# Attention backward loop: one transposing transfer per block of four units in place of two

## The chip, the cores and the metric

The kernel runs on one core of a Trainium2 chip. A core has engines that run side by side, each with its own in-order instruction stream: PE (TensorE, matmuls; PEld is its weight load), DVE (VectorE), ACT (ScalarE), POOL (GpSimd) and SP (SyncE, used here only to issue DMA transfers). They meet through semaphores. Sixteen DMA engines move data for all of them. The metric is the device time of one execution in microseconds (us).

## The reference

The kernel computes a transformer block with adaptive layer norm, forward and backward: the output and nine gradients, for 2048 tokens of width 512, in bfloat16. Forward, attention has 32 heads of 16 columns. Cut to what matters here:

```python
x = A_x
h = _layernorm(x) * (1 + ca) + sa
scores = einsum('bhqd,bhkd->bhqk', q, k) * Dh ** (-0.5)
p = softmax(scores);  o = einsum('bhqk,bhkd->bhqd', p, v)
x = x + ga * (o @ wo)
...
_out, _vjp = jax.vjp(_f, A_x, A_wqkv, A_wo, ...)
_grads = _vjp(grad_out)
```

The change lies in the backward pass of the attention. For a head, with E the exponentials of the scores and dO the gradient of o, it needs dS = E * (dO V^T - row term), and from it dK (dS transposed times Q), dV (E transposed times dO) and dQ (dS times K). As dS stands, with 128 queries on the partitions, PE can contract it over queries for dK. For dQ it must contract over keys, and for that dS has to be transposed.

## The kernel before

The program has three phases: the forward pass with the dense layers (to about 1115 us of the profile), the attention backward loop (to about 2388 us), and the input gradients and weight gradients (to the end). The change touches only the loop.

**Units and blocks.** A unit is four heads (head group hg, 8 of them) by 512 keys (kc, 4) by 128 queries (qc and qi, 4 by 4): `units`, line 1554, 512 in all. Four units that differ only in qi form a block, of which there are 128; block b holds units 4b to 4b+3. A head group has 16 blocks.

**What is done for a unit.** `score` (line 1587): four matmuls, one for each head, into one of three score banks of PSUM (A, B, C). `expo` (1597): four exponentials on ACT, from the banks into tile E_u. `dp_pair` (1602), twice: two matmuls into psD_u, then one DVE product (1616) that writes half of the unit's dS. `k_quad` (1648) and `v_quad` (1657): four matmuls each for dK and dV. `transpose_unit` (1623) issues the transposing transfers of dS from SP.

**What is done for a block.** Tile dsT holds the block's dS transposed, [128 keys, 4 units, 16 tiles, 128 queries]. `dq_quad` (1673, matmuls on line 1681) reads it, four times for a block, each over all four units at once; then `dq_out` (1684) evicts and adds up dQ.

**Two kinds of blocks.** In an even block all four units are transposed by DMA. In an odd block (`on_pe`, 1620) the fourth unit is transposed by PE (`pe_turn`, 1640, line 1644) and copied into dsT by ACT (1760), and only three go by DMA.

**Tiles and buffers.** A dS tile holds two units and has four buffers (1608, `cur["dS"]`); dsT has three buffers (1549). The tile framework puts in the waits: a new tile waits until the old one in its buffer has been read. A transfer reads 0.5 MB for each unit. In `transpose_unit` an even block makes two transfers of two units each, after its second and after its fourth unit (line 1631); an odd block makes one of two units after its second (1631), and one of one unit after its third (1629).

**The order.** It is written out by hand: in every round b the tokens of `order_t` (1705) or `order_n` (1710) are issued to the engines, and each engine follows that order. In round b: "s" and "e" are scores and exponentials of block b; "D" is a `dp_pair`, which runs one block behind or less: a block's fourth unit is finished by the first D that does work in the round after its own; "q" the dK and dV matmuls; "t" and "T" the PE transposes and copies of block b-1; "d1" and "d2" the `dq_quad`s of block b-2, in the second half of the round; "Q" its `dq_out`. A transposing transfer is issued right behind the D that completes its last unit. `order_t` runs when block b-1 is odd.

**Queues.** In the loop SP issues the transposing transfers, and in the last head group also five loads of 512 KB for the next phase (`load_grads`, 1546). ACT issues the loads for the next head group and the stores of finished gradients (`load`, 1576), one every four D's: 22 loads for each head group, and the stores. SP and ACT transfers draw their completion semaphores from the same eight. After the loop SP goes on with the loads of the last phase (1778 and after).

```python
            elif qi % 2 == 1:
                SP.dma_start(out=dqt[u // 4][:, qi - 1:qi + 1].rearrange("p u b q -> p (u b) q"),
                             in_=cur["dS"].rearrange("p u h k -> p (u h k)"), transpose=True)
```

Of the kernel before, what the change touches and what calls it, by code (L numbers as in the profile page):

```python
# [17 lines left out]
BF = dt.bfloat16  # L18
F32 = dt.float32

P = 128
# [13 lines left out]
def kernel(  # L35
# [21 lines left out]
    SP = nc.sync  # L57
# [89 lines left out]
    with ExitStack() as ph:  # L147
# [4 lines left out]
        ework = att.enter_context(tc.tile_pool(name="phCe", bufs=4))  # L152
# [1393 lines left out]
        SP.dma_start(out=tile_ap, in_=(dQc if key == "dq" else dVKtP)[i])  # L1546

    with ExitStack() as ph:
        tpool = ph.enter_context(tc.tile_pool(name="phIt", bufs=3))
        ework = ph.enter_context(tc.tile_pool(name="phIe", bufs=4))  # L1550
        wk = ph.enter_context(tc.tile_pool(name="phIw", bufs=2))
        psd = ph.enter_context(tc.tile_pool(name="psId", bufs=2, space=bass.MemoryType.PSUM))
# [3 lines left out]
        hst, bst, sst, dqt, cur = {}, {}, {}, {}, {}  # L1556
# [45 lines left out]
        def dp_pair(u, pair):  # L1602
            hg, kc, qc, qi = units[u]
            st = hst[hg]
            qt = qc * 4 + qi
            if pair == 0:
                if qi % 2 == 0:
                    cur["dS"] = ework.tile([P, 2, 4, 512], BF, name="dS_u", tag="dS_u", bufs=4)
                bst[u][1] = cur["dS"][:, qi % 2]
            E_u, dS_u = bst[u]  # L1610
            psD = psd.tile([P, 2, 512], F32, name="psD_u", tag="pd")
            for hi in range(2):
                r = 32 * (2 * pair + hi)
                PE.matmul(psD[:, hi, :], st["do"][r:r + 32, qt * P:(qt + 1) * P], st["v"][r:r + 32, kc * 512:kc * 512 + 512],  # L1614
                          start=True, stop=True, tile_position=(r, 0))
            DVE.tensor_tensor(dS_u[:, 2 * pair:2 * pair + 2, :], psD[:], E_u[:, 2 * pair:2 * pair + 2, :], ALU.mult)  # L1616
            if qi == 3 and on_pe(u // 4):
                held["dS"] = dS_u

        def on_pe(b):  # L1620
            return b % 2 == 1

        def transpose_unit(u):
            hg, kc, qc, qi = units[u]
            if qi == 0:
                dqt[u // 4] = tpool.tile([P, 4, 16, P], BF, name="dsT", tag="dsT")
            if on_pe(u // 4) and qi >= 2:
                if qi == 2:
                    SP.dma_start(out=dqt[u // 4][:, qi], in_=bst[u][1].rearrange("p h k -> p (h k)"), transpose=True)
            elif qi % 2 == 1:  # L1630
                SP.dma_start(out=dqt[u // 4][:, qi - 1:qi + 1].rearrange("p u b q -> p (u b) q"),
                             in_=cur["dS"].rearrange("p u h k -> p (u h k)"), transpose=True)

        held = {}

# [84 lines left out]
        with tc.manual_schedule(engines={PE.engine, ACT.engine, DVE.engine, SP.engine, POOL.engine}):  # L1720
# [4 lines left out]
            for b in range(NU // 4 + 3):  # L1725
                toks, bank = order_t if on_pe(b - 1) else order_n
                for tok in toks:
# [12 lines left out]
                    elif c == "D":  # L1740
                        if 0 <= nD < 2 * NU:
                            dp_pair(nD // 2, nD % 2)
                            if nD % 2 == 1:
                                transpose_unit(nD // 2)
                        nD += 1
                        cur["j"] = nD
                        for j in sorted(j for j in todo if j <= nD):
                            for f, args in todo.pop(j):
                                f(*args)
                    elif c == "q":  # L1750
                        if 0 <= nq < 2 * NU:
                            (v_quad if nq % 2 else k_quad)(nq // 2)
                        nq += 1
                    elif c == "f" and 0 < nq < 2 * NU:
                        keep_warm()
                    elif c == "t" and 0 <= b - 1 < NU // 4:
                        pe_turn(b - 1, i - 1)
                    elif c == "T" and 0 <= b - 1 < NU // 4:
                        dst, pt = held.pop(i - 1)
                        ACT.activation(dst, pt[:], AF.Identity)  # L1760
                    elif c == "d" and 0 <= b - 2 < NU // 4:
                        for kt in (2 * i - 2, 2 * i - 1):
                            dq_quad(b - 2, kt)
                    elif c == "Q" and 0 <= b - 2 < NU // 4:
                        dq_out(b - 2)
# [3 lines left out]
    with ExitStack() as ph:  # L1769
# [139 lines left out]
        with tc.manual_schedule(engines={PE.engine, ACT.engine, DVE.engine}):  # L1909
# [33 lines left out]
            for b in range(3):  # L1943
                for ic in range(DC):
# [8 lines left out]
                    elif i <= 2 * DC:  # L1953
                        k, h = (i - 1) // 2, (i - 1) % 2
# [67 lines left out]
```

## Time and profile before

| | |
|---|---|
| time, median of 3 runs | 2492.1 us (2487.35, 2492.10, 2492.11) |
| profiled execution, span | 2501.3 us |
| backward loop in it | about 1115 to 2388 us, 128 blocks |
| DVE product for dS, line 1616 | 1024 x 1.218 us |
| ACT exponential, line 1600 | 2048, some 0.65 us each, started every 0.48 us |
| transposing issue of two units, line 1631 | 192 |
| transposing issue of one unit, line 1629 | 64 |
| share of SP's DMA queue (q1) in the bytes moved | 389.35 of 437.70 MB |

How to read it: the busy rows say how much of the span each engine worked. The page cuts the span into 40 slices of 62.5 us and gives a digit for tenths busy. PEclk is the clock granted to TensorE, in tenths of full speed. The stretches view gives the same for any window, with the number of instructions in brackets. Its DMA share is a sum over packets, which overlap, and so can be above 1. In the view by tile a row gives the shortest, median and longest duration in ns and the first and last start in us. A row on "SPq" is SP's queue issuing a transfer; its duration is the time that SP is held by the issue, not the time until the data has landed. In the chain of waits a row gives start, duration and what the chain ran through; "DMA out<-in" there runs from the issue to the semaphore that released the waiting engine. Lines of the timeline that are alike and follow each other closely are merged (x3), with their whole extent as duration.

### The profile page before, as it was taken

To read this page: it belongs to the slowest core of one execution; us is meant where nothing else is said; L and a number is where in the kernel's file an instruction comes from. 1 tells how busy PE (TensorE), PEld (TensorE's weight loads), DVE (VectorE), ACT (ScalarE), POOL (GpSimd) and SP (SyncE) were. 2 spreads that over 40 slices of the span, in tenths; PEclk is the share of its full clock that TensorE was granted. 3 is DMA by queue.
4 is the path that set the end of the run, shared out by engine and by line. 5 is a ranking of instruction groups with operands and counts; after the bars stand their busy time and mean duration, and the time that the engine had idled before them with its cause. 6 is when DMAs were issued, how large, how long until landed. Compare 5 with 4: busy or idle time off the path is not lost.

```text
span 2501.3 us, 49888 instructions
## 1 busy us (share of the span) xinstructions
PE 2324.0 (93%) x18948; PEld 783.4 (31%) x19036; DVE 1837.7 (73%) x2377; ACT 2303.7 (92%) x3560; POOL 488.0 (20%) x661
## 2 busy tenths in 40 slices
PE   8899899989998998999999999999999999999989
PEld 3232233223332333443223323233232323332344
DVE  6555354455435444579989999999999999999965
ACT  7999999999998999539999999999999999999944
POOL 2111223323533453110111101111011110110100
PEclk9999999999998999999999999999999999999999
DMA  4468463258546865979999999999999999999984
GB/s 146 130 167 176 144 150 97 88 166 142 98 95 142 151 131 110 256 200 196 201 192 206 199 198 202 196 204 203 205 205 198 205 202 199 200 198 214 201 253 133
DMA packets 1189503, 437.70 MB, mean 175 GB/s; under 512 B 1065867, under 2 KB 1160521, under 8 KB 1188878
## 3 DMA queue, kind: packets, MB, share of 16 engines
q1 hardware_dynamic: 1152414, 389.35, 79.0%
q0 software_dynamic: 19872, 27.09, 6.5%
q10 hardware_dynamic: 16976, 18.07, 2.9%
q8 instruction: 149, 2.44, 0.4%
q14 instruction: 92, 0.75, 0.1%
HBM read 98.30 MB, written 70.80 MB: 68 GB/s over the span
## 4 chain that ended last, share of the span: by engine, by line
ACT 40%; PE 38%; issue 8%; DVE 7%; DMA 3%; SPq 1%; ACTq 1%; POOL 0%; DVEq 0%; another core or an unknown queue 0%; POOLq 0%
ACT E_u L1600 24%; ACT ET L578 12%; PE dqacc L1681 4%; PE psST L576 3%; PE psS_A L1594 3%; PE accVK L1654 2%; PE pm L233 2%; ACT dsT L1760 2%; PE psS_B L1594 2%; PE pdh L1858 2%; PE oacc L592 2%; PE psS_C L1594 2%; PE pwq L1892 2%; PE pm L500 2%; PE pm L410 2%
## 5 line engine op out<-in xcount | busy, mean ns | idle before, releaser
L1616 DVE TENSOR_TENSOR dS_u<-psD_u,E_u 128x1024 bf16<-128x1024 f32 x1024 | 1185.9, 1218 | 77.1 <-PE psD_u L1614 30.2
L578 ACT ACTIVATE ET<-psST 128x1024 bf16<-128x1024 f32 x1024 | 941.9, 1242 | 16.6 <-PE psST L576 16.3
L1600 ACT ACTIVATE E_u<-psS_A 128x512 bf16<-128x512 f32 x768 | 509.9, 664 | 10.8 <-PE psS_C L1594 8.5
L1600 ACT ACTIVATE E_u<-psS_B 128x512 bf16<-128x512 f32 x768 | 503.2, 655 | 10.8 <-DMA dsT<-dS_u 2.7
L1614 PE MATMUL psD_u<-iv,ido 32*128 32x512 bf16 x2048 | 409.1, 388 | 1.5 <-DVE dS_u L1616 1.3
L576 PE MATMUL psST<-qt_sb,kt_sb 32*128 32x512 bf16 x2048 | 313.8, 386 | 48.0 <-ACT ET L578 41.0
L1600 ACT ACTIVATE E_u<-psS_C 128x512 bf16<-128x512 f32 x512 | 334.3, 653 | 3.1 <-PE psS_B L1594 1.1
L1594 PE MATMUL psS_B<-ik,iq 32*128 32x512 bf16 x768 | 296.1, 386 | 11.7 <-ACT E_u L1600 4.4
L1594 PE MATMUL psS_A<-ik,iq 32*128 32x512 bf16 x768 | 294.5, 383 | 11.0 <-DVE dwlast L237 1.0
L1699 POOL TENSOR_TENSOR dQacc<-dQacc,dqtmp 128x512 f32<-128x512 f32 x64 | 81.2, 1268 | 858.8 <-ACT dqtmp L1694 797.4
L1594 PEld LDWEIGHTS <-iq 32*128 32x128 bf16 x2048 | 129.7, 91 | 313.9 <-issue 296.9
L1654 PE MATMUL accVK<-dS_u,qz 128*32 128x512 bf16 x2048 | 213.5, 388 | 0.5 <-PE psD_u L1614 0.2
L592 PE MATMUL oacc<-ET,vaug 128*32 128x512 bf16 x2048 | 207.0, 394 | 3.9 <-DVE ostage L596 3.9
L1663 PE MATMUL accVK<-E_u,dOs_tok 128*16 128x512 bf16 x2048 | 204.5, 388 | 0.0
L1594 PE MATMUL psS_C<-ik,iq 32*128 32x512 bf16 x512 | 194.2, 379 | 4.5
L576 PEld LDWEIGHTS <-kt_sb 32*128 32x128 bf16 x2048 | 84.3, 91 | 328.2 <-issue 306.5
L1681 PE MATMUL dqacc<-dsT,KS_tok 128*32 128x512 bf16 x2048 | 145.7, 382 | 18.8 <-DMA dsT<-dS_u 5.0
L1760 ACT ACTIVATE dsT<-ptT 128x1024 bf16<-128x1024 bf16 x128 | 144.1, 1126 | 13.1 <-PE ptT L1644 12.2
L251 DVE COPY part<-pm 128x512 f32<-128x512 f32 (+2 forms) x106 | 65.2, 615 | 121.9 <-PE pm L233 111.8
L1614 PEld LDWEIGHTS <-ido 32*128 32x128 bf16 x2048 | 105.2, 91 | 101.3 <-issue 94.9
L1654 PEld LDWEIGHTS <-qz 128*32 128x32 bf16 x2048 | 58.5, 94 | 178.0 <-issue 162.9
L1699 POOL TENSOR_TENSOR dQst<-dQacc,dqtmp 128x512 bf16<-128x512 f32 x32 | 40.6, 1270 | 266.1 <-ACT dqtmp L1694 266.1
(415 smaller groups left out, 2688.7 us busy)
## 6 DMA issues: line engine op xcount, KB each, us to landing
p_st<-part POOLq DMA_DIRECT2D x36, 256.0 KB, 4.6
kt_sb<-qkT_st POOLq DMA_DIRECT2D x124, 64.0 KB, 3.0
wA<-in_B_w_dram SPq DMA_DIRECT2D x28, 256.0 KB
wB<-w1T_st SPq DMA_DIRECT2D x21, 256.0 KB
wA<-w2T_st SPq DMA_DIRECT2D x21, 256.0 KB
wB<-in_B_w_dram SPq DMA_DIRECT2D x21, 256.0 KB
p_st<-part POOLq DMA_DIRECT2D x28, 192.0 KB, 4.6
p_st<-part SPq DMA_DIRECT2D x18, 256.0 KB
```

What stands on the lines that cost most here:

```text
L576: PE.matmul(ps[:, hi, :], kt_sb[r:r + 32, kt * P:(kt + 1) * P], qt_sb[r:r + 32, :], start=True, stop=True, tile_position=(r, 0))
L578: ACT.activation(ET[:, 2 * pair:2 * pair + 2, :], ps[:], AF.Exp, scale=SCALE)
L592: PE.matmul(oacc[32 * hq:32 * hq + 32, :], lhsT, ET[:, hq, :], start=(kt == 0), stop=(kt == TT - 1), tile_position=(0, 32 * hq), skip_grou ...
L1594: PE.matmul(psS[:], st["q"][r:r + 32, qt * P:(qt + 1) * P], st["k"][r:r + 32, kc * 512:kc * 512 + 512], start=True, stop=True, tile_positi ...
L1600: ACT.activation(bst[u][0][:, hq, :], sst.pop((u, hq))[:], AF.Exp, scale=SCALE)
L1614: PE.matmul(psD[:, hi, :], st["do"][r:r + 32, qt * P:(qt + 1) * P], st["v"][r:r + 32, kc * 512:kc * 512 + 512], start=True, stop=True, til ...
L1616: DVE.tensor_tensor(dS_u[:, 2 * pair:2 * pair + 2, :], psD[:], E_u[:, 2 * pair:2 * pair + 2, :], ALU.mult)
L1654: PE.matmul(cur["vk"][32 * hq:32 * hq + 32, :], hst[hg]["qz"][:, qt, hq, :], bst[u][1][:, hq, :], start=(qt == 0), stop=False, tile_positi ...
L1663: PE.matmul(acc[32 * hq:32 * hq + DH, :], dOs_tok[:, qt, (hg * 4 + hq) * DH:(hg * 4 + hq + 1) * DH], E_u[:, hq, :], start=False, stop=(qt ...
L1681: PE.matmul(acc[32 * hq:32 * hq + 32, :], KS_tok[:, kc * 4 + kt, h * DH:h * DH + 32], tT[:, :, hq * 4 + kt, :], start=(kt == 0), stop=(kt ...
L1699: POOL.tensor_tensor(dst2, dst, tmp[:], ALU.add)
L1760: ACT.activation(dst, pt[:], AF.Identity)
```

## The change

An even block makes one transfer of four units after its fourth; an odd block makes one of three units after its third. The fourth unit of an odd block still goes by PE and ACT. The dS tile grows from two units to four and has three buffers in place of four (12 units in place of 8); dsT has two buffers in place of three, and is taken when the transfer is issued, not at the block's first unit. Sizes in SBUF: dS 4 x 8 KB becomes 3 x 16 KB a partition, dsT 3 x 16 KB becomes 2 x 16 KB. The bytes moved, the matmuls, the exponentials and the order are as before.

```diff
@@ -1546,7 +1546,7 @@
-        tpool = ph.enter_context(tc.tile_pool(name="phIt", bufs=3))
+        tpool = ph.enter_context(tc.tile_pool(name="phIt", bufs=2))
@@ -1604,9 +1604,9 @@
             if pair == 0:
-                if qi % 2 == 0:
-                    cur["dS"] = ework.tile([P, 2, 4, 512], BF, name="dS_u", tag="dS_u", bufs=4)
-                bst[u][1] = cur["dS"][:, qi % 2]
+                if qi == 0:
+                    cur["dS"] = ework.tile([P, 4, 4, 512], BF, name="dS_u", tag="dS_u", bufs=3)
+                bst[u][1] = cur["dS"][:, qi]
@@ -1622,14 +1622,11 @@
         def transpose_unit(u):
             hg, kc, qc, qi = units[u]
-            if qi == 0:
+            w = 3 if on_pe(u // 4) else 4
+            if qi == w - 1:
                 dqt[u // 4] = tpool.tile([P, 4, 16, P], BF, name="dsT", tag="dsT")
-            if on_pe(u // 4) and qi >= 2:
-                if qi == 2:
-                    SP.dma_start(out=dqt[u // 4][:, qi], in_=bst[u][1].rearrange("p h k -> p (h k)"), transpose=True)
-            elif qi % 2 == 1:
-                SP.dma_start(out=dqt[u // 4][:, qi - 1:qi + 1].rearrange("p u b q -> p (u b) q"),
-                             in_=cur["dS"].rearrange("p u h k -> p (u h k)"), transpose=True)
+                SP.dma_start(out=dqt[u // 4][:, 0:w].rearrange("p u b q -> p (u b) q"),
+                             in_=cur["dS"][:, 0:w].rearrange("p u h k -> p (u h k)"), transpose=True)
```

## The prediction

> **What bounds the kernel now.** I began on the page with busy time and queues.
>
> ```profile
> PE 2324.0 (93%) x18948; PEld 783.4 (31%) x19036; DVE 1837.7 (73%) x2377; ACT 2303.7 (92%) x3560; POOL 488.0 (20%) x661
> PEclk9999999999998999999999999999999999999999
> DMA  4468463258546865979999999999999999999984
> q1 hardware_dynamic: 1152414, 389.35, 79.0%
> ```
>
> From slice 18 on, the backward loop, DMA is at nine tenths, nearly all of it on SP's queue, q1. So I asked for busy time by stretch, one row for 200 us of the loop and three for two blocks each.
>
> ```profile
> core 0: us, PE busy (x) PEld busy (x) DVE busy (x) ACT busy (x) POOL busy (x), PEclk, DMA share, GB/s
> 1573.50:1592.60 19.10, 18.39 (x181) 5.87 (x180) 18.33 (x17) 18.88 (x37) 2.54 (x2) 1.00 1.10 200
> 1631.60:1651.00 19.40, 18.85 (x181) 5.97 (x180) 18.60 (x17) 19.36 (x39) 0.00 (x0) 1.00 1.26 183
> 1766.90:1789.90 23.00, 19.85 (x181) 5.71 (x180) 18.88 (x17) 19.17 (x37) 0.00 (x0) 0.93 1.14 208
> 1500.00:1700.00 200.00, 192.47 (x1869) 60.65 (x1870) 190.40 (x165) 197.26 (x376) 27.04 (x19) 1.00 1.20 202
> ```
>
> ACT (exponentials, L1600) is busy 197.26 of 200 us and sets the pace. Two blocks take 19.1 to 19.4 us where nothing disturbs them; PE and DVE have less than 1 us to spare in that, so a lost us is not caught up. Next the instructions that issue the transposing transfers, and SP's timeline in a quiet and a crowded stretch (start, duration).
>
> ```profile
> L1631 SPq DMA_TRANSPOSE dsT<-dS_u x192: 4766/5266/6831, 1123.7 to 2377.1; - x192
> L1629 SPq DMA_TRANSPOSE dsT<-dS_u x64: 1759/2336/4402, 1140.0 to 2382.1; - x64
> ...
> 1580.68 15.59 SPq L1631 DMA_TRANSPOSE dsT<-dS_u  x3
> 1596.33 1.76 SPq L1629 DMA_TRANSPOSE dsT<-dS_u  x1
> ...
> 1640.62 18.26 SPq L1631 DMA_TRANSPOSE dsT<-dS_u  x3
> 1658.98 2.83 SPq L1629 DMA_TRANSPOSE dsT<-dS_u  x1
> ```
>
> An issue occupies SP for about as long as the data stream, and the four issues of two blocks follow each other: 17.4 us in quiet (15.59 + 1.76), 21.1 in the crowd (18.26 + 2.83, while ACT's loads share the DMA engines), against a period of 19.2. Over all pairs of blocks the four issues sum to 16.9 at least, 18.3 in the median, 20.0 at the ninetieth percentile. SP is a second engine at its limit. Last, the chain of waits where the transfers reach the path.
>
> ```profile
> 1677.73 6.81 DMA dsT<-dS_u
> 1684.54 0.14 issue
> 1684.67 0.61 PE dqacc L1681 x8
> ...
> 1767.47 9.73 DMA dsT<-dS_u
> 1777.20 0.02 issue
> 1777.22 0.32 ACTq L1576
> ```
>
> At 1684.54 a single-unit transfer lands just as PE needs it. At 1777.20 ACT, about to issue a load, has waited for a transfer that held that load's semaphore. So the path is ACT's, with the transfers close beneath.
>
> **The change, part by part.**
>
> *Timing of a block.* I took from the trace, for each block, the end of DVE's last product in a transfer (ready), the issue, the last update of the transfer's semaphore (landed), and the first L1681 matmul (needed). Medians: an even block is needed 14.06 us after its fourth unit is ready, an odd one 14.60 after its third; the odd block is ready 6.79 after the even one before it. Now the second transfer of a block lands with 5.1 (even) and 4.7 us (odd) to spare, because the first half is long under way.
>
> *Later issue.* The first half loses its head start. Quiet case, blocks 46 and 47: the fourth unit of 46 is ready at 1585.64; today its second issue takes 4.95 and lands 2.0 after. In one piece the issue takes 5.00 + 4.95, to 1595.6, and lands at 1597.6; needed at 1599.61: 2.0 left. Block 47, ready at 1592.43, queues behind until 1595.6, takes 5.42 + 1.76, to 1602.8, lands 2.6 after, at 1605.4; needed at 1607.03: 1.6 left. In medians for even blocks: two pair issues of 5.3 and a lag of 2.8 make 13.4 against 14.06. So about 4 us of cover become 0.6 to 2.0, and a crowd (3.7 us more in the example) takes more than that.
>
> *Sum over the loop.* I recomputed the queue for all 128 blocks: ready and needed as measured, issues and lags as measured, the two issues of a block joined, the five SP loads of the last head (L1546) left where they are, and whatever comes late moves all behind it. With joining free of gain or loss, 44 blocks come late and the loop grows by 34.6 us; if joining saves 0.2 us a block, 24.4; 0.3, 20.2; 0.8, 6.5; 1.2, 2.9; if it costs 0.25, 51.3; 0.5, 71.1. No row has three or four units, so this saving is the unknown. Lower side: in unbroken queues a pair lands 5.40 us after its predecessor (66 cases) and a single 2.45 (50), so two singles are cheaper than a pair by 0.5. Upper side: around each landing the packet record of q1 shows about 1 us with almost no packet, followed by some 2 us at 1133 packets/us in place of 850, which wins back two thirds; at most 1.2 could be saved. I take 0.2, nearer to the landings, since they include the winning back. PE and ACT may swallow some of a wait: with 0.25 us swallowed 24.4 becomes 18.9. I take **22**.
>
> *Fewer transfers.* Per two blocks two instructions leave SP. Their gaps (1580.68 + 5.00 to 1585.73) are 0.05 us, nothing. Semaphores come round after eight transfers of SP and ACT together, so ACT's loads find older ones: the wait at 1777.20 should go. That stretch took 23.0 in place of 19.3: **-3** (between 0, if another load falls in its place, and -3.7).
>
> *Clock.* Behind that 2.7 us stop the granted clock reads 0.5 for 3.4 us (0.93 over the stretch), and of the 3.7 us lost 1.0 is more than the stop. Of the late blocks at 0.2 nine are later than 1 us, one above 1.4 (2.7): between 0 and 9; I take **+3**. The Trainium skill, TensorE: Matmul & The Clock Gate, HAM oscillation, wants "no PE-idle gaps >~3.4µs", longer than any stop here; this trace shows half clock after less, and by the page alone the sum would be 3 lower.
>
> *Buffers.* dsT with two buffers makes SP wait, before a transfer, for L1681 of two blocks earlier; behind it on SP stand only the next transfers. Block 44's last L1681 ended at 1581.47, 4.2 before 1585.64; block 45's at 1589.17, 6.4 before 1595.6. DVE's first write into a dS tile waits for the transfer of three blocks earlier; behind it are DVE's later products, then PE. Block 49 writes first at 1604.80, 7.2 after 1597.6; block 50 at 1614.21, 8.8 after 1605.4. Both stops shift with the loop, so the cover holds: 0, and at worst the same lateness a second time, inside the range. ACT's copies (L1760) and PE's turn of the fourth unit do not move.
>
> *End of the loop.* SP's last issue ends at 2384.00, and the loads of the next phase stand behind it on the path (L1778, then qz). In the recomputed queue it ends there plus the loop's growth: nothing to add.
>
> Sum: 22 - 3 + 3 = +22. The profiled execution has 2501.3, so 2523; the median of the runs is 9.2 lower, and with that kept: **2514 us**.
>
> **The rivals.**
>
> *Not slower: joining removes the dip.* If descriptors of one transfer stream through and the empty microsecond goes, a block saves 0.8 to 1.2: +6.5 or +2.9, less 3.7 for ACT's wait, with no stop long enough for the clock: 2491 to 2495; with 0.5 swallowed per stop, 2490. For it: the empty microseconds are real. Against: the fast stretch behind them, and 5.40 against twice 2.45. It decides from a saving of about 0.7. The Trainium skill, DMA: Bandwidth & Descriptors, Anatomy of one DMA, gives a transfer (there from GpSimd's queue) some 2.0 us of fixed cost; taken as stream time that would be this rival in full, but a chained single lands in 2.45 for a quarter of a block, which leaves 0.45 for the data.
>
> *Much slower: the queue becomes the pace.* If long transfers cost 0.25 to 0.5 more per block (the landings' lower bound), +51 to +71: 2543 to 2563. Against: quiet stretches need 17.4 of 19.2 and have room.
>
> *Swallowed.* If PE and ACT hide a whole microsecond of every wait, 7.9 remain at 0.2, less 3: 2497. For it: three score banks ahead of ACT. Against: blocks 117 to 121 now have 0.1 to 0.4 us to spare and two stretches there took 20.4 and 19.5, not 19.2.
>
> **How the numbers follow.** The runs before spread over 4.8 us, so 0.2% (5 us) is what tells from no change. Forecast, slower by 8 to 40: 0.62. Dip removed: 0.18, of it same 0.11, faster 0.07 (runs without any half clock behind a stop). Queue as pace: 0.13. Swallowed: 0.07, half of it same. Faster 0.08 with a remainder, same 0.15, slower 0.77. The forecast's own range is 2500 to 2532; the whole one runs from the dip removed to the middle of the queue as pace, 2490 to 2553.
>
> **What would show it.** Right: L1681 waits for DMA dsT<-dS_u dozens of times, not three; two issues per two blocks of about 10 and 7.5 us; two-block stretches of 20 us where loads are under way and 19.2 where not; SP idle before each even block. Wrong: issues clearly under 9.5 and 7.0 (the dip goes), or quiet stretches over 19.5 (the queue is the pace), or DVE waiting for dS_u's buffer.

## The result and the profile after

The changed kernel takes 2529.7 us (median, 2525.3 to 2533.1) against 2491.7 (2487.4 to 2492.1): 1.0161 times as long, 95% interval 1.0141 to 1.0181. That is 38 us slower, inside the range on record (2490 to 2553), 16 above the 2514 predicted. Its profiled execution has a span of 2528.4 us.

The page of the changed kernel: busy time, the granted clock and DMA by slice, SP's queue, and the chain of waits by engine.

```profile
PE 2327.7 (92%) x18948; PEld 780.3 (31%) x19036; DVE 1839.4 (73%) x2377; ACT 2303.6 (91%) x3560; POOL 488.8 (19%) x661
...
PEclk9999999999998999999999999999999999999999
DMA  4567453368546847969999999999999999999994
...
q1 hardware_dynamic: 1148318, 389.33, 77.0%
...
PE 36%; ACT 33%; DMA 15%; issue 7%; DVE 7%; POOL 0%; ACTq 0%; SPq 0%; another core or an unknown queue 0%; DVEq 0%; POOLq 0%
```

The same row of the chain in the kernel before:

```profile
ACT 40%; PE 38%; issue 8%; DVE 7%; DMA 3%; SPq 1%; ACTq 1%; POOL 0%; DVEq 0%; another core or an unknown queue 0%; POOLq 0%
```

The work is the same to within 4 us on every engine, and so are the bytes (389.33 against 389.35 MB on SP's queue). What changed is who is waited for: DMA makes up 15% of the chain that ends last, before the change 3%.

The stretches view of the changed kernel: two blocks in quiet, two of the costliest pairs, and 200 us.

```profile
core 0: us, PE busy (x) PEld busy (x) DVE busy (x) ACT busy (x) POOL busy (x), PEclk, DMA share, GB/s
1574.30:1593.40 19.10, 18.39 (x181) 5.87 (x180) 18.29 (x17) 18.88 (x37) 2.54 (x2) 1.00 1.03 194
1612.80:1638.30 25.50, 20.69 (x185) 5.95 (x184) 19.28 (x17) 19.55 (x38) 0.00 (x0) 0.87 1.14 200
1776.00:1802.00 26.00, 20.79 (x185) 5.92 (x184) 19.37 (x17) 19.54 (x37) 0.00 (x0) 0.80 1.17 196
1500.00:1700.00 200.00, 184.98 (x1765) 56.53 (x1758) 181.66 (x157) 187.37 (x359) 25.78 (x18) 0.97 1.11 196
```

Quiet pairs of blocks take 19.1 us as before. The loss sits in single pairs of 20 to 26 us, some with a lower granted clock. ACT, busy 197.26 of 200 us before, is busy 187.37.

The issues, by tile (shortest, median and longest in ns):

```profile
L1628 SPq DMA_TRANSPOSE dsT<-dS_u x128: 7216/9628/11398, 1126.5 to 2407.3; - x128
```

Split by kind of block, the medians are 9.89 us for four units and 7.76 for three (blocks 4 to 125, as in all medians by block below). Who waited for whom in the changed kernel between 1150 and 2380 us (total, times, longest):

```profile
PEld L1678 <- DMA dsT<-dS_u: 36.3, 36, 3.2
PE dqacc L1678 <- DMA dsT<-dS_u: 18.4, 23, 2.6
ACT E_u L1600 <- DMA dsT<-dS_u: 8.3, 2, 4.4
```

The same view of the kernel before:

```profile
ACT E_u L1600 <- DMA dsT<-dS_u: 2.7, 1, 2.7
PEld L1681 <- DMA dsT<-dS_u: 1.0, 3, 0.5
PE dqacc L1681 <- DMA dsT<-dS_u: 0.7, 2, 0.4
```

Two waits have grown. The first is the predicted one: the dQ matmuls (L1678 is the old L1681, three lines up) stand for a block that has not landed. Its PEld row is a wait of the weight load, during which PE can still be at work, so the two rows are not to be added up as lost time. The second was predicted to go and has grown: ACT stands for a transposing transfer that it does not read at all. The chain of waits of the changed kernel shows that one (start, duration).

```profile
1616.03 13.32 DMA dsT<-dS_u
1629.36 0.02 issue
1629.38 0.34 ACTq L1576
...
1629.82 0.61 ACT E_u L1600
```

At 1629.38 ACT issues a load of the next head's q. It takes semaphore 101, which the three-unit transfer of block 49, issued at 1616.03, has held until 1629.36. ACT's instructions run in order, so the exponentials behind the load wait too.

### The profile page after: what moved, and what is told of

It reads as the page before. It is cut to its first block, busy times and chain, and to the rows that moved or that the text cites. A ratio compares the mean times of both kernels' runs of the same rounds, so it can differ in the third digit from the quotient of the medians.

```text
span 2528.4 us, 49362 instructions
## 1 busy us (share of the span) xinstructions
PE 2327.7 (92%) x18948; PEld 780.3 (31%) x19036; DVE 1839.4 (73%) x2377; ACT 2303.6 (91%) x3560; POOL 488.8 (19%) x661
## 3 DMA queue, kind: packets, MB, share of 16 engines
q1 hardware_dynamic: 1148318, 389.33, 77.0%
## 4 chain that ended last, share of the span: by engine, by line
PE 36%; ACT 33%; DMA 15%; issue 7%; DVE 7%; POOL 0%; ACTq 0%; SPq 0%; another core or an unknown queue 0%; DVEq 0%; POOLq 0%
ACT E_u L1600 17%; DMA dsT<-dS_u 14%; ACT ET L578 13%; PE dqacc L1678 4%; PE psST L576 3%; PE psS_A L1594 2%; PE pm L233 2%; PE accVK L1651 2%; PE psS_B L1594 2%; PE oacc L592 2%; PE pwq L1889 2%; PE pdh L1855 2%; PE pm L424 2%; PE pm L500 2%; PE pm L410 2%
## 5 line engine op out<-in xcount | busy, mean ns | idle before, releaser
L578 ACT ACTIVATE ET<-psST 128x1024 bf16<-128x1024 f32 x1024 | 941.5, 1298 | 13.3 <-PE psST L576 13.0
L1600 ACT ACTIVATE E_u<-psS_B 128x512 bf16<-128x512 f32 x768 | 501.9, 654 | 34.1 <-PE psD_u L1614 16.1
L1678 PE MATMUL dqacc<-dsT,KS_tok 128*32 128x512 bf16 x2048 | 153.0, 398 | 37.6 <-DMA dsT<-dS_u 24.7
```

Of the source, the lines that this page charges most:

```text
L578: ACT.activation(ET[:, 2 * pair:2 * pair + 2, :], ps[:], AF.Exp, scale=SCALE)
L1600: ACT.activation(bst[u][0][:, hq, :], sst.pop((u, hq))[:], AF.Exp, scale=SCALE)
L1678: PE.matmul(acc[32 * hq:32 * hq + 32, :], KS_tok[:, kc * 4 + kt, h * DH:h * DH + 32], tT[:, :, hq * 4 + kt, :], start=(kt == 0), stop=(kt ...
```

## The experiments

"Loop" below runs from the first exponential of block 2 to that of block 126. "Stores" are the seven pairs of blocks, one at each head's end, in which ACT issues the four dQ stores beside its loads (blocks 18, 34, 50, 66, 82, 98, 114 and the next). In e2, e9, e10 and e12 the stores are spread over this pair and the next one, so there the column holds two of the four. "Half clock" is the time in the loop at a granted clock of 0.5; it comes in steps of 3.4 us. "Late" counts, of the 122 blocks 4 to 125, those whose first dQ matmul starts less than 0.3 us after landing. These columns come from one profiled execution each, and that can be an extreme one: e7's is the fastest of its ten runs (2481.0 us), e11's the slowest of its ten (2514.2). The ratio is from the timed runs; it is taken to all runs of the kernel before that there were by then (medians 2489.6 to 2491.7), so it is not quite the quotient of the column of medians.

| kernel | median us | ratio, 95% | loop us | stores us | half clock us | late |
|---|---|---|---|---|---|---|
| before | 2491.7 | 1 | 1218.6 | 143.1 | 47.8 | 5 |
| changed | 2529.7 | 1.0161 [1.0141, 1.0181] | 1249.2 | 161.1 | 68.3 | 31 |
| e1 two transfers | 2493.7 | 1.0015 [0.9996, 1.0035] | 1211.3 | 139.5 | 30.7 | 7 |
| e2 spread stores | 2523.4 | 1.0122 [1.0094, 1.0151] | 1238.6 | 138.2 | 51.2 | 39 |
| e3 changed, loads on POOL | 2546.2 | 1.0220 [1.0201, 1.0239] | 1262.8 | 171.1 | 85.3 | |
| e4 before, loads on POOL | 2509.9 | 1.0083 [1.0066, 1.0100] | 1227.4 | 157.6 | 44.4 | |
| e5 halves issued last | 2493.8 | 1.0010 [0.9991, 1.0029] | 1210.7 | 138.4 | 23.9 | 12 |
| e6 even blocks joined | 2551.6 | 1.0244 [1.0221, 1.0268] | 1265.0 | 176.7 | 81.9 | 37 |
| e7 odd blocks joined | 2487.1 | 0.9990 [0.9973, 1.0007] | 1202.8 | 140.5 | 6.8 | 3 |
| e8 one per unit | 2517.5 | 1.0105 [1.0078, 1.0133] | 1234.3 | 138.8 | 64.9 | 13 |
| e9 halves held back | 2541.9 | 1.0198 [1.0168, 1.0228] | 1255.8 | 140.0 | 78.5 | 40 |
| e10 e6, spread stores | 2519.1 | 1.0104 [1.0071, 1.0136] | 1227.4 | 135.5 | 27.3 | 46 |
| e11 few loads | 2504.7 | 1.0046 [1.0023, 1.0068] | 1231.2 | 145.5 | 81.9 | 24 |
| e12 e7, spread stores | 2504.0 | 1.0051 [1.0033, 1.0068] | 1224.0 | 144.3 | 34.1 | 2 |

**e1: the new tiles alone.** Two transfers per block as before, in the new tiles. The kernels e5 to e10 and e12 are made from this one: e6, e7 and e8 by its list of parts alone, the others as said there.

```diff
-            if qi == w - 1:
-                dqt[u // 4] = tpool.tile(...)
-                SP.dma_start(out=dqt[u // 4][:, 0:w]..., in_=cur["dS"][:, 0:w]..., transpose=True)
+            for lo, hi in (((0, 2), (2, 3)) if on_pe(u // 4) else ((0, 2), (2, 4))):
+                if qi != hi - 1:
+                    continue
+                if lo == 0:
+                    dqt[u // 4] = tpool.tile(...)
+                SP.dma_start(out=dqt[u // 4][:, lo:hi]..., in_=cur["dS"][:, lo:hi]..., transpose=True)
```

> The new tiles (three dS tiles of four units, two dsT tiles) with the two transfers per block of before. Late-transfer theory and semaphore theory: both go back to before, 2487 to 2497 us, L1681 waits for dsT no more than about 3 to 6 times. Rival, the buffers cost the time: stays above 2510 us, with waits of SP or DVE for a buffer.

Level with before. The waits of e1, same view and window:

```profile
PE dqacc L1681 <- DMA dsT<-dS_u: 7.7, 5, 5.1
PEld L1681 <- DMA dsT<-dS_u: 2.2, 2, 1.3
```

The one wait of 5.1 us comes at 2377.9, at the end of the loop, where the kernel before has 4.4. So neither the larger dS tile nor the two dsT buffers cost the 38 us; the transfers do. The two buffers are not free, though: a block's first transfer must now wait until PE has read the block two before it (SP's waits at L1631 end with PE some 120 times in e1, never in the kernel before). A block lands 10.2 (even) and 12.0 us (odd) after it is ready, before the change 9.1 and 10.1; needed at 14.0 and 14.6, it is still in time.

**e2: ACT's stores apart.** The changed kernel with one line edited:

```diff
-                    at(cur["j"] + 6 + hq, load, dQc[...], st["dq"][...])
+                    at(cur["j"] + 6 + 8 * hq, load, dQc[...], st["dq"][...])
```

> The changed kernel, with ACT's four dQ stores at a head's end eight D apart in place of one D apart, so that ACT's transfers no longer come round the eight semaphores within one transposing transfer. In the trace of the changed kernel the seven stretches of two blocks with these stores took 161.1 us, before 143.1: 18.0 of the loop's growth of 30.6. Semaphore theory: some 10 to 16 us come back, 2513 to 2520 us, and ACT no longer stops for a dsT transfer of 3 to 4 us. If only late transfers count: 2527 to 2532 us, unchanged.

ACT no longer stops for a transposing transfer, and the seven store pairs fall from 161.1 to 138.2 us, the level of e1. But the rest of the loop grows by 12, with 39 late blocks; 6 of the 12 are in the pairs just behind, which now hold the other two stores (142.3 to 148.6). By medians 6 us come back, a little less than expected; the two intervals just meet, so this run alone does not settle it. e10 does.

**e3 and e4: loads and stores issued by POOL**, in the changed kernel and in the one before.

```diff
         def load(to, fro):
-            ACT.dma_start(out=to, in_=fro)
+            POOL.dma_start(out=to, in_=fro)
```

> The changed kernel with ACT's loads and stores of the loop issued by POOL, so that ACT waits for no transfer's semaphore at all; the bytes and their times are as before. Semaphore theory: 2508 to 2518 us, ACT waits for DMA dsT 0 us, L1681 still waits for dsT some 20 to 40 times. If only late transfers count: 2527 to 2532 us.

> The kernel before with ACT's loads and stores of the loop issued by POOL. Semaphore theory: the one stop of 2.7 us and its half clock go, and the smaller waits of the stores: 2483 to 2490 us. If ACT's waits for semaphores are hidden: 2490 to 2494 us.

Both miss: 17 and 18 us slower, not faster. The timeline of SP in e4 (start, duration) tells why:

```profile
1751.65 20.88 SPq L1631 DMA_TRANSPOSE dsT<-dS_u  x3
1772.58 6.67 SPq L1629 DMA_TRANSPOSE dsT<-dS_u  x1
1779.35 15.76 SPq L1631 DMA_TRANSPOSE dsT<-dS_u  x3
```

Between 1761.1 and 1767.5 POOL issues eleven loads and stores in a row; in the kernel before, ACT issues the same eleven between 1765.1 and 1798.3. The transposing issues in that time stretch to 20.88 + 6.67 us for two blocks, against 15.76 + 1.78 in the next pair. So these runs say nothing of ACT's semaphore waits. They show that loads issued by POOL make the transfers late, in either kernel. Whether that is the bunching is not shown: the loads also change their queue (in e4 14.4 MB have gone from q10, hardware_dynamic, to q0, software_dynamic).

**e5: both halves asked for at the block's end.** In e1, the condition becomes `if qi != w - 1`.

> The new tiles, two transfers per block as before, but both issued when the block's last unit is ready. If the lost head start costs the time: 2520 to 2540 us, like the changed kernel. If it is the long single transfer (its semaphore, its pace): back at 2490 to 2500 us.

2493.8 us, but the experiment did not do what it was to do. SP has nothing else in its queue, and the first half waits only for its own two units: in the trace it is still issued 2.6 us (median, even blocks) ahead of the last unit. A transfer that is asked for later in the order is not held back by that when its queue is idle. e9 repairs this.

**e6 and e7: one kind of block joined.** The parts are ((0, 4),) with ((0, 2), (2, 3)) in e6, and ((0, 2), (2, 4)) with ((0, 3),) in e7.

> Only even blocks have one transfer of four units; odd ones keep two and one. Head start theory: the odd block's first half, ready 4.5 us after the even block, still queues behind the four units until 9.7, so both blocks land as late as in the changed kernel: 2512 to 2528 us. If each joined block costs by itself: about half, 2505 to 2512 us.

> Only odd blocks have one transfer of three units; even ones keep two and two. Head start theory: the even block's second half is issued by 5.3 us after its ready time, the odd block at 6.8 without a queue, lands near 17 and is needed at 21.4, so nothing is late: 2488 to 2498 us. If each joined block costs by itself: 2505 to 2512 us.

e7 came out as expected: 3 late blocks, level with before. e6 is slower than the whole change, which neither case had. Its waits between 1150 and 2380 us:

```profile
ACT E_u L1600 <- DMA dsT<-dS_u: 26.1, 6, 5.3
PEld L1681 <- DMA dsT<-dS_u: 22.5, 28, 2.7
PE dqacc L1681 <- DMA dsT<-dS_u: 21.5, 26, 2.4
```

The lower two rows are the late blocks, as in the changed kernel. The upper one is ACT's stop, at each of six head ends, behind a load whose semaphore an odd block's transfer still holds (9.2 to 10.7 us from issue to landing). In the changed kernel two loads did so at full length. Whether a load draws a semaphore that is still held depends on how the eight come round: e7, also with three transfers for two blocks, has no such stop, and neither has e1.

**e8: one transfer for each unit.** Parts of one unit each.

> The new tiles, one transfer for each unit as soon as it is ready (seven issues for two blocks). If a transfer has hardly any fixed cost and an earlier start helps: 2484 to 2495 us, no L1681 wait for dsT. If a transfer costs about 0.7 us of the queue by itself: 7 issues need over 19.3 us for two blocks, 2510 us or more. ACT's loads find a semaphore of a recent transfer more often: ACT waits in the stretches with stores, up to 10 us in all.

24 us slower than e1, though each unit starts as soon as it is ready. Of this 12.0 us are idle time of ACT behind eighteen waits for semaphores; the blocks land 1.2 (odd) to 1.4 us (even) later than in e1, with 13 late. Fixed cost and semaphores are mixed here, so it is no measure of either.

**e9: the halves really held back.** In e1, the parts are turned round and asked for at the block's end, ((2, 4), (0, 2)) and ((2, 3), (0, 2)), so that the part with the last unit is first in SP's queue and the other one stands behind it; ACT's stores are apart as in e2.

> The new tiles, two transfers per block, the half with the last unit first, so that SP's order holds both back until the block's last unit is ready; ACT's stores eight D apart, which keeps the semaphore wait out. Head start theory: as late as e2, 2513 to 2530 us, L1681 waits for dsT 20 times or more. If a long single transfer is needed for the loss: 2487 to 2497 us, few waits.

2541.9 us, above the range expected and 48 us above e1, with the same two transfers per block. First issue 0.03 us behind the last unit, 40 blocks late, no ACT stop. Its waits:

```profile
PE dqacc L1681 <- DMA dsT<-dS_u: 32.1, 25, 2.7
PEld L1681 <- DMA dsT<-dS_u: 14.9, 10, 3.3
```

So the late start costs by itself, without any joining. Not all of the 48 us is the late start: moving the stores alone costs 17 us where hardly a block is late (e12 beside e7). Beside e2, which starts as late, has its stores in the same places and differs in joining (and in the order of the parts), e9 is 18.5 us slower: joining gives something back. From a block's first issue to its landing the medians are 13.47 (four units) and 11.20 (three) in the two parts of e9, 13.09 and 10.93 joined in e2, and 13.25 and 11.00 in the changed kernel: 0.2 to 0.4 us a block.

**e10: e6 with the stores apart.**

> e6 with ACT's stores eight D apart. In e6's trace ACT stood 26.1 us behind six loads whose semaphore a transposing transfer still held, and six half clocks of about 1.3 us may follow: semaphore theory: 25 to 35 us come back, 2516 to 2527 us, level with e2. If the even block's long transfer itself made e6 slow: 2545 us or more.

2519.1 us, as expected: 32.5 us come back, and the row of ACT is gone, with the late blocks still there:

```profile
PEld L1681 <- DMA dsT<-dS_u: 24.2, 32, 1.6
PE dqacc L1681 <- DMA dsT<-dS_u: 21.2, 32, 2.2
```

One line that moves three stores by 8 to 25 us removes ACT's stop; that settles what it is. It also removes 16 of 24 half clocks (81.9 to 27.3 us).

**e11: fewer loads.** The loads of head groups 2 to 7 are left out of the changed kernel; these groups compute with the tiles of groups 0 and 1.

```diff
-            for i, (to, fro) in enumerate(loads):
+            for i, (to, fro) in enumerate(loads if hg == 1 else []):
```

> The changed kernel without ACT's loads for head groups 2 to 7 (these groups compute with the tiles of groups 0 and 1; the stores stay). Crowd theory: the cover of 0.6 to 2.0 us of quiet stretches is enough, L1681 waits for dsT fewer than 10 times, 2488 to 2500 us. If the late start is too late by itself: 2515 us or more.

2504.7 us: 25 of 38 us come back, less than expected, and 24 blocks are still late where fewer than 10 were expected, 20 of them odd. For 18 of those 20 the even block before had landed with 0.9 us or more to spare: an odd block can be late behind an undisturbed even one. What the 25 us are is only in part shown. Without the loads both the crowd and ACT's stops are gone (no ACT wait for a transposing transfer is left), and the kernel before was not run without its loads. Pairs of blocks without a half clock take 19.31 us (mean), as in the kernel before (19.34; the changed kernel has 19.56). PE's idle time ahead of the dQ matmuls falls from 27.5 to 17.8 us, the kernel before has 6.2. So leaving out the loads takes away about half of the growth in these waits, and the other half stays.

**e12: e7 with the stores apart.**

> e7 (one transfer of three units in odd blocks, two of two in even ones) with ACT's stores eight D apart. e7 had no semaphore wait left in its trace, so nothing more to gain from it: 2482 to 2492 us, between 0.3% faster than before and the same.

A miss: 17 us slower than e7. Two blocks are late, but at the first six head ends the two pairs of blocks that hold the stores take 20.3 to 22.2 us, where e7 has 19.3 to 20.1 and once, with a half clock, 21.1. ACT idles 0.3 to 0.4 us behind two of the four stores, and a half clock follows some. Moving the stores helps where ACT would stop for 4 us and harms where it would not; so the 6 us that e2 gains are what is left of the stop's cost after that harm. No kernel here beats the one before clearly; e7, at 0.9990 [0.9973, 1.0007], is level with it.

## Why the prediction held, and where it was off

**Later issue.** Right. A block has 14.1 (even) and 14.6 us (odd) from ready to needed; it now lands 13.3 and 14.3 us after ready (medians), predicted for even blocks 13.4. 31 blocks come late, and ahead of seven PE stands for more than 1 us, where nine were forecast. PE's idle time ahead of the dQ matmuls grew from 6.2 to 27.5 us: 21 against a term of 22. e9 shows the cause without joining, e7 that an odd block can wait for its third unit as long as the even one keeps its head start, e11 that some half of the waiting stays when the loads are gone.

**The saving of joining**, taken as 0.2 us a block between -0.5 and 1.2, measured 0.2 to 0.4 (the changed kernel and e2, each against e9). So the rival by which the dip goes, 0.8 to 1.2, falls: by its own test the issues would be under 9.5 and 7.0 us, and they are 9.89 and 7.76. The fixed 2.0 us that the Trainium skill gives a transfer from GpSimd (DMA: Bandwidth & Descriptors, Anatomy of one DMA) is not time of this stream: one transfer less for each block saves 0.2 to 0.4. The queue as pace falls too: quiet pairs still take 19.1 to 19.4 us. Swallowing falls with the 21 us of PE idle.

**Fewer transfers, -3: the step that failed.** I reasoned that with two SP transfers in place of four, ACT would find older semaphores. That leaves out that a transfer now holds its semaphore for 13.2 us (four units) or 10.9 (three), in place of 8.0 to 8.4 (two) and 5.1 (one; medians from issue to landing), and that ACT issues eight transfers in one pair of blocks at a head's end, so that a whole round of eight semaphores passes within one transfer. ACT's stop grew from 2.7 to 8.3 us, and the seven store pairs from 143.1 to 161.1. e10 shows what such stops cost in all: 32 us for 26.1 us of stops in e6. In the changed kernel the share is smaller: 6 us or somewhat more by medians (e2), against a gain of 3 predicted. The transfer that stood at 1777.20 before the change was itself a dQ store, the fourth, and not a load.

**Clock, +3.** Half clock in the loop went from 47.8 to 68.3 us, six steps of 3.4. A pair of blocks with one step takes 20.6 us in the kernel before (without the pair of the 2.7 us stop), without one 19.3 (means): 1.25 us each, some 7.5 in all by this estimate, within the 0 to 9 given. Behind ACT's stops of 4 us it is there each time (clock 0.87 and 0.80 in the stretches above, and at all six stops of e6). PE's gaps in the two stops of the changed kernel are 3.85 and 4.27 us. The rule of 3.4 us of idle PE (the Trainium skill, TensorE: Matmul & The Clock Gate, HAM oscillation) agrees with these in length; yet in the second the clock falls 0.8 us after the gap begins. Of the fourteen steps before the change, thirteen have no PE gap over 1 us near them (from 6 us before a step's start to 1 us behind it), so that one step behind a stop, from which the term was read, could have been chance. Of the twenty after it, nine have none: eleven lie at such a gap, and there the term had the mechanism right. What brings the others is open.

**The median.** My sum for the profiled execution was 2523, measured 2528.4. To get a median I kept the 9.2 us by which the profiled execution before was slower than the timed runs. The changed kernel's profiled execution is 1.3 under its median. The one before was an unlucky one: fourteen half clocks, where e1, of the same pace, had nine and e7, in its fastest run, two. Five fewer would be 6 of the 9 us, by the estimate above. So of the 16 us that the prediction is short, about 10 are this offset and 5 are the sum. The 5 can't be split cleanly. The measured terms, 21 + 6 + 7.5, make 34.5, and the loop grew by 30.6: half clocks behind ACT's stops are in both the 6 and the 7.5. The part ahead of the loop was 3 us shorter in the profile after, though its code is the same. The one term with the wrong sign is that of the semaphores.

**Buffers and end of the loop, 0.** Right: e1 is level, DVE never waits for a dS buffer and SP not for a dsT buffer, and from block 126 on the profile has 143.9 us, before 144.4.

## What to carry to other kernels

Joining two transfers on a full queue saves the cost of one transfer, here 0.2 to 0.4 us a block, and costs the first one's head start, here 4 us; it pays only where the head start is not needed, so work out ready, landed and needed for each block before joining. A longer transfer also holds its completion semaphore longer: look for what on the critical engine takes the next round of it. And compare a predicted profile with a profile, and count the half clocks in both, before carrying an offset to the median.

## What was not expected of the hardware

The half clock comes with stops and also without any. Over the kernels above it takes 6.8 to 85.3 us of the loop, 2 to 25 steps, at about 1.25 us of loss each; e10 with 46 late blocks has 8 steps, e11 with 24 late blocks 24. Of e9's 23 steps four have no PE gap over 1 us near them, of the changed kernel's 20 nine, of the 14 before the change thirteen. Within one execution all stretches of half clock begin on one grid of 3.41 us, whatever lies ahead of them; so it is in the traces of the kernel before, the changed one and e6.

Eleven loads and stores issued within 6.4 us by POOL (e4) stretch one transposing issue of two units from about 5.3 to 9.28 us.
